# One 1024-wide spectra product, skip term and one block's sums moved to TensorE, quadrant first stages and a tabled order in an S4D and SwiGLU kernel

## The chip, the cores and the metric

The kernel runs on one core of a Trainium2 chip. A core has TensorE (matrix products, PE in the profile), VectorE (DVE), ScalarE (ACT), GpSimd (POOL) and SyncE (SP), which issues most of the DMAs. Each engine works through its own list of instructions in order and waits at semaphores for the others. The metric is the time of one execution on the device in microseconds, lower being better.

## What is computed

x has 2048 positions and 640 channels. The first half convolves a normalised x along its positions with a kernel K that is generated from 128 complex exponentials per channel; the second half is a gated feed-forward. What matters of the reference:

```python
P = jnp.exp((A * dt[:, None])[:, :, None] * pos[None, None, :])
K = 2.0 * jnp.einsum("dn,dnl->dl", C, P).real
Kf = jnp.fft.rfft(K, L2)                      # L2 = 4096
Uf = jnp.fft.rfft(u_t, L2)
y = jnp.fft.irfft(Uf * Kf[None, :, :], L2)[:, :, :L]
return y + u * D_skip[None, None, :]
...
h = _layernorm(x, axis=-1) * (1 + ca) + sa
x = x + ga * _A_ref(h, ...)
h = _layernorm(x, axis=-1) * (1 + cb) + sb
x = x + gb * _B_ref(h, B_w1, B_w3, B_w2)      # silu(h w1) * (h w3), then w2
```

## The kernel before

The channels are taken in five blocks b of 128. All matrix products of the convolution are in fp32, each of them two instructions of TensorE, and an FFT of 4096 points is written as two stages of small products. For each block the kernel does this:

- **The generator**, eight chunks c of 16 channels (`gen_tasks`, `gen_chunk`). GpSimd adds phases (ph) and multiplies tables of exponentials (yy, xx; the tables are in the tiles e of even blocks and `late` of odd ones). ScalarE takes the sines into PSUM (tr). VectorE multiplies the two (five operations, 512 or 1024 wide). TensorE multiplies xx and yy into kps, 32 products of 64 columns. ScalarE copies kps into ks, and VectorE then adds the skip term D_skip (tile dsk) to one column in 64 of it, a 128x4 operation (`skip`). kps has two halves of one PSUM bank, taken in turn.
- **The normalised input** (`h_tasks`): four tiles hn are made by ScalarE or VectorE (four 128x128 operations each), multiplied and added to by VectorE (hb), and sent through DRAM (hs) into xb.
- **The first stage**, of xb and of ks (`first_tasks`): 8 groups each of 8 products of 128 rows and 128 moving columns, into the PSUM tile ps; ScalarE or VectorE copies it into the spectrum sp (or sp2). The constant matrix wk is zero outside two blocks of 64 rows by 64 columns.
- **The spectra** (`spectra_tasks`), 8 steps i: TensorE makes fh and fk, the second stages of the input and of the kernel, in PSUM. ScalarE copies fh into hz (SBUF). VectorE multiplies fk by the real part of hz into the tile fp (SBUF), and by the imaginary part into fk itself, in place (PSUM), 512 wide each. Two 256-wide operations then subtract and add the second product from and to the first (`both`: fp is input and output, fk the other input). After two steps the inverse stage fz is two products with wz for each half f, copied into zt by ScalarE or VectorE and stored to DRAM (zd).

A fifth block's spectra are followed by the tail: the last inverse stage of the first half (iz, izb, loaded from zd; iy, iyb on TensorE), the second normalisation, and the feed-forward, which runs from about 400 us to the end, in fp32r products.

**The order.** Each piece of work is a task that `Plan.add` registers with its engine (or two, the first being preferred), its assumed duration, the tasks that it follows, and the buffers that it takes and gives. `Plan.place` (from line 188) simulates the engines with these durations and a rank per task, read from the table RANKS, and the instructions are then emitted in the order of that simulation. The flag `port` marks tasks that the simulation keeps from running on VectorE and GpSimd at once. Nothing but this emitted order and the waits decides what runs when. The feed-forward (`ffn`, `groups`, `late`) is emitted after the plan, by plain loops.

**Lines.** In the trace most of the plan's instructions are put down to L157, a helper's line, so groups are told apart by the tiles' names.

Of the kernel before, what the change touches and what calls it, by code (L numbers as in the profile page):

```python
# [29 lines left out]
EXPS = ((0, 0, 0, 64.0), (0, 1, 0, 1.0), (1, 0, 0, 512.0), (1, 1, 4, 8.0), (1, 2, 0, 8.0))  # L30
# [3 lines left out]
RANKS = """  # L34
# [65 lines left out]
"""  # L100
FP = 2
EPS = 1e-5
MAGIC = 1.5 * 2.0 ** 23
REV = float(2 ** 32 - 256)
# [2071 lines left out]
```

## Time and profile before

| | before |
|---|---|
| median of 3 runs | 972.96 us (972.6 to 973.78) |
| the profiled execution | 972.31 us |
| its span, first to last instruction | 970.5 us |
| PE busy | 859.9 us, 89% |
| DVE busy | 702.0 us, 72% |
| ACT busy | 546.4 us, 56% |
| POOL busy | 340.5 us, 35% |
| mean granted TensorE clock | 0.975 |

A group's row reads: line, engine, operation, output and inputs by the program's names, shapes, count | busy time, mean of one in ns | the engine's idle time just before them, and what ended it. A row of the timeline reads: start and duration in us, engine, line, operation, count, and in brackets the idle time before it with what ended it. A row of the stretches gives busy times (and counts) of PE, PE's weight loads, DVE, ACT and POOL, then the granted clock, the DMA engines' busy share and GB/s. The shares of the table are averages over stages of different kinds.

### The profile page before, as it was taken

How to read it: one execution, taken by the hardware profiler on the slowest of the kernel's cores; microseconds unless marked ns; L12 is line 12 of the kernel's file. 1: busy time of each engine (PE TensorE's matmuls, PEld its weight loads, DVE VectorE, ACT ScalarE, POOL GpSimd, SP SyncE). 2: the span in 40 equal slices, each digit the busy share in tenths (PEclk: the TensorE clock that was granted, in tenths of full speed). 3: DMA queues.
4: the chain of work that ended last, by engine and by line, in shares of the span. 5: the costliest groups of instructions: out<-in, count | busy, mean ns of one | idle time of the engine just before them, and what ended most of it. 6: DMA issues, size and time to landing. Idle time of an engine off the chain costs nothing.

```text
span 970.5 us, 20551 instructions
## 1 busy us (share of the span) xinstructions
PE 859.9 (89%) x7985; PEld 681.8 (70%) x7985; DVE 702.0 (72%) x1395; ACT 546.4 (56%) x1022; POOL 340.5 (35%) x371
## 2 busy tenths in 40 slices
PE   1464787889899997899999999999999999999997
PEld 1132665767778884677777778888788888888775
DVE  7998899999999968886767677557456464645422
ACT  6877788979888851564434455346444344443412
POOL 1797889879799600002111111000011212120000
PEclk9996999999999999799999999999999999999999
DMA  9955453723425268935434422276342322220374
GB/s 218 275 168 191 111 136 95 177 66 106 111 80 152 74 159 206 241 118 182 122 120 139 122 96 68 82 209 194 112 134 64 102 77 86 82 82 28 108 220 133
DMA packets 110506, 127.31 MB, mean 131 GB/s; under 512 B 10568, under 2 KB 90696, under 8 KB 109128
## 3 DMA queue, kind: packets, MB, share of 16 engines
q1 hardware_dynamic: 109032, 125.21, 45.3%
q8 instruction: 63, 1.03, 0.5%
q10 hardware_dynamic: 1376, 0.79, 0.3%
q14 instruction: 35, 0.29, 0.1%
HBM read 95.82 MB, written 30.15 MB: 130 GB/s over the span
## 4 chain that ended last, share of the span: by engine, by line
PE 70%; DVE 17%; ACT 5%; issue 4%; DMA 3%; POOL 1%; SPq 1%; ACTq 0%; DVEq 0%
PE c L157 19%; PE acc L157 18%; PE X L157 12%; PE ps L157 4%; PE gu L157 3%; DVE yy L157 3%; PE kps L157 3%; PE fz L157 2%; PE fk L157 2%; DVE fp L157 2%; PE fh L157 2%; DVE hn L157 2%; DVE xx L157 2%; DVE xb L157 1%; ACT tr L157 1%
## 5 line engine op out<-in xcount | busy, mean ns | idle before, releaser
L157 PE MATMUL acc<-ah,w 128*128 128x512 f32 x560 | 173.2, 395 | 2.4 <-DMA w<-w2d 1.7
L157 PEld LDWEIGHTS acc<-ah,w 128*128 128x128 f32 x560 | 103.7, 188 | 26.4 <-issue 2.1
L157 PE MATMUL acc<-al,w 128*128 128x512 f32 x260 | 102.4, 394 | 0.0
L665 DVE TENSOR_TENSOR wl<-s,wh 128x256 fp32r<-128x256 f32 x92 | 38.9, 423 | 67.5 <-ACT wh L664 67.1
L841 POOL TENSOR_TENSOR s<-wr 128x256 f32<-128x256 f32 x22 | 16.4, 744 | 187.8 <-DMA wr<-in_w 94.8
L157 POOL TENSOR_TENSOR ph<-p,p 128x1024 int32<-128x1024 int32 x40 | 79.2, 1979 | 8.2 <-ACT tr L157 8.0
L664 ACT ACTIVATE wh<-s 128x256 fp32r<-128x256 f32 x92 | 37.6, 410 | 78.5 <-PE X L157 58.1
L157 PE MATMUL kps<-yy,xx 128*32 128x64 f32 x2560 | 51.8, 234 | 28.6 <-DVE xx L157 21.4
L157 DVE TENSOR_TENSOR yy<-yy,tr 128x512 f32<-128x512 f32 (+1 forms) x80 | 75.3, 943 | 1.2 <-ACT tr L157 0.6
L157 PEld LDWEIGHTS kps<-yy,xx 128*32 128x32 f32 x2560 | 45.1, 116 | 38.3 <-issue 22.0
L664 ACT ACTIVATE wh<-wr 128x256 fp32r<-128x256 f32 x92 | 38.4, 418 | 56.0 <-PE X L157 42.3
L842 POOL TENSOR_TENSOR s<-s,wr 128x256 f32<-128x256 f32 x22 | 16.6, 755 | 134.0 <-issue 133.9
L902 ACT ACTIVATE t<-g 128x512 f32<-128x512 f32 x44 | 27.8, 632 | 52.7 <-DVE g L866 52.7
L157 ACT ACTIVATE tr<-ph,hpi 128x512 f32<-128x512 f32 x80 | 54.6, 690 | 4.4 <-DVE xx L157 2.7
L157 PEld LDWEIGHTS acc<-al,w 128*128 128x128 f32 x260 | 48.9, 188 | 10.8 <-DVE al L665 0.3
L871 DVE SCALAR_TENSOR_TENSOR g<-t,g 128x512 f32<-128x512 f32 x48 | 33.7, 702 | 31.3 <-ACT t L902 29.3
L157 POOL TENSOR_TENSOR yy<-e,e 128x512 f32<-128x512 f32 x48 | 52.4, 1109 | 8.8 <-PE kps L157 5.9
L157 DVE TENSOR_TENSOR xx<-tr,xx 128x512 f32<-128x512 f32 x80 | 54.3, 680 | 1.1 <-ACT tr L157 1.1
L157 PE MATMUL ps<-wk,ks 128*64 128x128 f32 x640 | 42.4, 285 | 13.6 <-DVE ks L157 8.9
L157 ACT ACTIVATE tr<-ph 128x512 f32<-128x512 int32 x80 | 47.3, 598 | 12.4 <-DVE yy L157 6.5
L157 PE MATMUL ps<-wk,xb 128*64 128x128 f32 x640 | 46.1, 295 | 6.3 <-ACT sp L157 3.0
L157 PEld LDWEIGHTS ps<-wk,ks 128*64 128x64 f32 x640 | 37.0, 143 | 20.3 <-ACT hn L157 6.6
(448 smaller groups left out, 2379.7 us busy)
## 6 DMA issues: line engine op xcount, KB each, us to landing
w<-w2d SPq DMA_DIRECT2D x42, 640.0 KB, 3.9
wr<-in_w SPq DMA_DIRECT2D x50, 320.0 KB, 3.9
zd<-zt SPq DMA_DIRECT2D x40, 256.0 KB, 2.9
w2d<-w SPq DMA_DIRECT2D x14, 640.0 KB, 3.5
xs<-in_x SPq DMA_DIRECT2D x16, 320.0 KB, 11.3
hs<-hb SPq DMA_DIRECT2D x20, 256.0 KB, 2.5
xb<-hs SPq DMA_DIRECT2D x20, 256.0 KB, 4.9
iz<-zd SPq DMA_DIRECT2D x32, 160.0 KB, 5.0
```

The source lines that it names most:

```text
L157: self.prev = self.k.order(f(*a, **kw), self.prev)
L664: self.nc.scalar.activation(H, v, AF.Copy)
L665: eng.tensor_tensor(Lo, v, H.bitcast(F32), op=ALU.subtract)
L841: eng.tensor_tensor(s[0], u[:, 0:2], u[:, 2:4], op=ALU.add)
L842: eng.tensor_tensor(s[1], s[0], g[:, 0:2], op=ALU.subtract)
L871: V.scalar_tensor_tensor(g, th, 1.0, g, op0=ALU.add, op1=ALU.mult)
L902: tanh = lambda o, i: A.activation(o, i, AF.Tanh, scale=0.5)
```

## The change

- **The product of the spectra** is one 1024-wide operation: fk (PSUM), read twice, times hz (SBUF), into the four planes of a tile fp twice as large. fk is not written to any more.
- **The sums** of blocks 1 to 4 (SUMS) stay two 256-wide operations of VectorE, now between planes of fp. Block 0 has none: its inverse stage has four products for each half instead of two, with a third column of wz for the minus sign.
- **The skip term** is a product of TensorE, the identity by dsk, added to kps. VectorE's `skip` is gone. kps is one buffer.
- **The first stages** use only the two blocks of wk that aren't zero: 4 groups each of 32 products of 64 rows and 64 columns, by row half h and real or imaginary part r, into two PSUM banks, and two copies of each group.
- **The al8 product** (b by j) is written into a part of the table e itself, and the exponentials end in place.
- **Loads.** The tiles of the first inverse rows (iz0, iz1) lie in sp2 and no longer wait for the memory change behind the generator.
- **The order** is a table, ORDER: entry n is the n-th task that the plan adds, and a mark (') takes its second engine. `Plan.place` is gone. Many assumed durations are changed, which has no effect now that nothing simulates them.

```diff
+SUMS = (1, 2, 3, 4)
...
-    wz = np.tile(np.stack([np.block([c, s]), np.block([-s, c])], 1), (2, 1, 1))
+    wz = np.tile(np.stack([np.block([c, s]), np.block([-s, c]), np.block([-c, -s])], 1), (2, 1, 1))
...
-    def place(self, rank):
+    def sequence(self):
...
+        for x in ORDER.split():
+            n = names[int(x.rstrip("'"))]
...
+            out.append((engs[x.endswith("'")], n))
...
+            nc.tensor.matmul(kps.rearrange("p (e b) -> p e b", b=64)[:, :, 63], self.ident, self.dsk[:, d0 // P, d0 % P // 4:d0 % P // 4 + 4],
+                             start=False, stop=True, skip_group_check=True)
...
-        def skip(c):
-            o = slice(4 * c, 4 * c + 4)
-            V.tensor_add(self.ks[b][:, o, 63], kps.pop(c).rearrange("p (e b) -> p e b", b=64)[:, :, 63], self.dsk[:, b, o])
...
-            for e in range(4):
-                x = self.ks[b][:, 4 * i + e, :] if m else xb[:, :, 4 * i + e]
+            for e in range(8):
+                x = self.ks[b][:, 8 * i + e, :] if m else xb[:, :, 8 * i + e]
                 for r in range(2):
...
-                    nc.tensor.matmul(o, x, self.wk[:, r, :], start=True, stop=True, tile_position=(0, 64 * r))
+                    for h in range(2):
+                        g = slice(64 * h, 64 * h + 64)
+                        o = pk[i, h][r * 64:(r + 1) * 64].rearrange("p (v j i f) -> p i j v f", j=2, i=8, f=2)[:, e]
+                        nc.tensor.matmul(o, x[g], self.wk[g, r, g], start=True, stop=True, tile_position=(64 * h, 64 * r))
...
-            k = bank[1, i]
-            to = k if r else prod[i // 2][:, :, i % 2 * 2:i % 2 * 2 + 2, :].rearrange("p r q d -> p q r d")
-            nc.vector.tensor_mul(to, k, bc(held[i][:, :, r], 2, 2))
+            k = bank.pop((1, i)).rearrange("p q r d -> p r (q d)")
+            h = held[i].rearrange("p q r d -> p r (q d)")
+            to = prod[i // 2][:, :, :, i % 2 * 2:i % 2 * 2 + 2, :].rearrange("p s r q d -> p s r (q d)")
+            nc.vector.tensor_mul(to, bc(k, 1, 2), bc(h, 2, 2))
...
-                p = prod[i // 2][:, r, i % 2 * 2:i % 2 * 2 + 2, :]
-                nc.vector.tensor_tensor(p, p, k[:, :, 1 - r], op=op)
+                nc.vector.tensor_tensor(p[:, 0, r], p[:, 0, r], p[:, 1, 1 - r], op=op)
...
+            terms = ((0, 0, 0), (0, 1, 1), (1, 1, 2), (1, 0, 1))[:2 if last else 4]
...
-            if b == 0:
-                x[0] = self.ks[0].rearrange("p e b -> p (e b)")[:, :1024]
-            else:
-                x[0] = self.xsp.tile([P, 4 * D], F32, name="xs_al8", tag="xs", bufs=4)[:, :1024] if b == 1 else self.fpool.tile([P, 1024], F32, name=f"al8{b}", tag="al8", bufs=1)
-            x[0] = x[0].rearrange("p (d j) -> p d j", j=8)
+            x[0] = E[0][:, :, 1, :]
...
+            t = s[:, :2048] if u == 0 else s[:, 2048:] if u == 1 else self.xb if u == 3 else self.ip.tile([P, 2048], F32, name="iz2")
```

More of the change, by code (lines that the diff above doesn't have):

```diff
@@ L168 @@
 class Plan:
-    LAG = dict(PE=0.2, DVE=0.18, ACT=0.2, POOL=0.15, SP=0.0)
-    CHAIN = dict(DVE=0.12, ACT=0.12, POOL=0.07)
-    NEAR, RATE, LAND, FLY, ISSUE, AWAY, TABLE = 0.1, 235e3, 1.3, 0.7, 0.06, 8, 1.28
     def __init__(self, **rings):
@@ L258, in place @@
+        taken, done, out = {r: [] for r in self.n}, set(), []
+        for x in ORDER.split():
+            n = names[int(x.rstrip("'"))]
+            engs, _, _, after, _, _, take, give, _, _ = T[n]
+            assert n not in done and done.issuperset(after), n
+            for r, y, _ in take:
+                i = len(taken[r]) - self.n[r]
+                assert i < 0 or not uses[r, taken[r][i]], n
+                taken[r].append(y)
             for k in give:
                 uses[k] -= 1
-                given[k] = max(fin + self.LAG.get(e, 0.0), given.get(k, 0.0))
@@ L261, in place @@
-                if not uses[k]:
-                    freed[k] = given[k]
-            for m in nexts[n]:
-                left[m] -= 1
-                if not left[m]:
-                    ready.append(m)
-        assert len(end) == len(T), ("never", [n for n in T if n not in end][:20])
-        return order
-    def run(self):
-        T = self.tasks
-        found = [int(x) for x in RANKS.split()]
-        searched = [n for n in T if n not in self.own]
-        assert len(found) == len(searched)
-        self.order = self.place({n: t[4] for n, t in T.items()} | dict(zip(searched, found)))
-        for s, f, e, n in self.order:
-            if T[n][2]:
-                T[n][2](e)
+            done.add(n)
@@ L282 @@
+            out.append((engs[x.endswith("'")], n))
+        assert len(done) == len(T)
+        return out
+    def run(self):
+        for e, n in self.sequence():
+            if self.tasks[n][2]:
+                self.tasks[n][2](e)
 class K:
@@ L1113, in dst @@
                         return z[u][pr][h * 64:h * 64 + 64]
-                    load(f"iz{u}.{pr}{h}", zv[:, t0:t0 + 2, :cut], dst, 262144, done + ([f"hh{b4}.{i}.m" for i in range(8)] if u > 2 else []))
+                    load(f"iz{u}.{pr}{h}", zv[:, t0:t0 + 2, :cut], dst, 262144, done + ([f"hh{b4}.{i}.m" for i in range(4)] if u > 2 else []),
+                         "inv" if u < 2 else "change")
         def load_up(m):
@@ L1169, in lo @@
                     self.low(h[:, :k], l[:, :k], x)
-                add(f"wh{m}.{i}", "ACT", .36, hi, names + (after[i:i + 1] if after else []), rank)
-                add(f"wl{m}.{i}", "DVE", .42, lo, [f"wh{m}.{i}"], rank)
+                add(f"wh{m}.{i}", "ACT", .32, hi, names + (after[i:i + 1] if after else []), rank)
+                add(f"wl{m}.{i}", "DVE", .34, lo, [f"wh{m}.{i}"], rank)
         def down_split(m, rank):
@@ L1175, in hi @@
                 w2[m] = self.w2_high(m, w2r[m])
-            add(f"w2h{m}", "ACT", .73, hi, [f"ld{m}.{i}" for i in range(1 if m < 13 else 2)], rank, take=[("w2", 1)])
-            add(f"w2l{m}", "DVE", .82, lambda: self.w2_low(m, w2r[m], w2[m]), [f"w2h{m}"] + (["ln1"] if m in (0, 13) else []), rank)
+            add(f"w2h{m}", "ACT", .66, hi, [f"ld{m}.{i}" for i in range(1 if m < 13 else 2)], rank, take=[("w2", 1)])
+            add(f"w2l{m}", "DVE", .74, lambda: self.w2_low(m, w2r[m], w2[m]), [f"w2h{m}"] + (["ln1"] if m in (0, 13) else []), rank)
             add(f"w2k{m}", "SP", 0, lambda: self.w2_keep(m, w2[m]), [f"w2l{m}", "izb1"], rank, dma=[655360],
@@ L1237, in prepare @@
             add(f"iyb{b}", "PE", 1.9, lambda: last_inv(b), [f"izb{b}", f"lwd{b}", "border"] + (["iyb0"] if b else []), 16.0, take=[("gu", 1)])
-            add(f"iab{b}", "DVE", .7, lambda: last_plus(b), [f"iyb{b}"] + [f"lx{b}.{q}" for q in range(4)], rank, give=[("gu", f"iyb{b}"), ("w2", f"izb{b}")])
-            add(f"isb{b}", "DVE", 1.15, lambda: last_stats(b), [f"iab{b}"], rank)
+            add(f"iab{b}", "DVE", .6, lambda: last_plus(b), [f"iyb{b}"] + [f"lx{b}.{q}" for q in range(4)], rank, give=[("gu", f"iyb{b}"), ("w2", f"izb{b}")])
+            add(f"isb{b}", "DVE", .78, lambda: last_stats(b), [f"iab{b}"], rank)
             steps = {}
@@ L1587, in inv @@
             self.sp2 = self.fpool.tile([P, 16, P, 2], F32, name="sp2")
-        plan.add("inv", None, 0, inv, ["cols", "mag1"], 0)
+        plan.add("inv", None, 0, inv, ["cols", "mag1", "hscalef", "colsf", "q0.v1", "q1.v1"] + [f"h0.{i}.a" for i in range(4)] + [f"k0.{i}.e{h}" for i in range(2) for h in range(2)] +
+                 [f"rw{g}" for g in range(4)], 0)
         self.early_tasks(e)
@@ L1613, in border @@
             self.x2 += [self.fp.tile([P, 4, D], F32, name=f"x2{i}") for i in (2, 3)]
-        plan.add("change", None, 0, change, [f"g{b}.7.p", f"g{b}.7.d"] + [f"h{b}.{i}.x" for i in range(4)], 0, own=True)
+        plan.add("change", None, 0, change, [f"g{b}.7.p", f"g{b}.7.r"] + [f"h{b}.{i}.x" for i in range(4)], 0, own=True)
         self.tail_tasks(border, cut)
@@ L1787, in gen_tasks @@
                     give=[("tr", n + f"s{(0, 0, 1, 3, 4)[i]}")])
-            add(n + "p", "PE", 1.1, lambda c=c: ch[c][4](), [n + f"m{i}" for i in range(5)], t + 3,
+            add(n + "p", "PE", 1.28, lambda c=c: ch[c][4](), [n + f"m{i}" for i in range(5)] + (["dsk"] if b == 0 else []), t + 3,
                 take=[("kg", 1)], give=[("yy", n + "z0"), ("xx", n + "z2")])
-            add(n + "r", "ACT", .27, lambda c=c: rows(c), [n + "p"] + ([f"k{b - 1}.{i}.m" for i in range(8)] if b else ["exp0", "q0.t0", "q1.t0"]), t + 3, give=[("kg", n + "p")])
-            add(n + "d", "DVE", .1, lambda c=c: skip(c), [n + "r"] + (["dsk"] if b == 0 else []), t + 3, give=[("kg", n + "p")])
+            add(n + "r", "ACT", .27, lambda c=c: rows(c), [n + "p"] + ([f"k{b - 1}.{i}.m" for i in range(4)] if b else ["exp0", "q0.t0", "q1.t0"]), t + 3, give=[("kg", n + "p")])
     def h_tasks(self, b):
@@ L1803, in h_tasks @@
             place = (lambda: self.pbank("hn")) if b else (lambda: self.psg.tile([P, 512], F32, name="hn", tag="f", bufs=3))
-            add(n + "n", ("ACT", "DVE"), (1.95, .85), lambda e, i=i, place=place: self.h_norm(b, i, place(), e), [n + "l", "hscale"], t, take=[(bank, 1)],
+            add(n + "n", ("ACT", "DVE"), (1.89, 1.66), lambda e, i=i, place=place: self.h_norm(b, i, place(), e), [n + "l", "hscale"], t, take=[(bank, 1)],
                 give=[("xq", n + "l")] if b else [])
@@ L1855, in spectra_tasks @@
         bank, prod, held = {}, {}, {}
-        four = lambda x: x.rearrange("p (q r d) -> p q r d", q=2, r=2)
+        last = b in SUMS
+        four = lambda x: x.rearrange("p (r q d) -> p q r d", q=2, r=2)
         def of(m, i):
@@ L1911, in spectra_tasks @@
             j = 4 * b + i // 2 - FP
[L1912 to L1913 removed]
+            first = [f"hh{b}.{x}.e{h}" for x in range(4) for h in range(2)] + (["wb", "cols", "inv"] if b == 0 else [])
+            firstk = [f"k{b}.{x}.e{h}" for x in range(4) for h in range(2)]
             if i or b == 0:
@@ L1925, in spectra_tasks @@
             j = i // 2
+            y = "c" if last else "x"
             n = f"z{b}.{j}."
-            add(n + "z", "PE", 1.95, lambda j=j: inverse(j), [f"w{b}.{i - 1}.c", f"w{b}.{i}.c"], t + W["late"], take=[("bank", 1), ("bank", 1, "'")],
-                give=[("fp", f"w{b}.{i - 1}.x0")])
+            add(n + "z", "PE", 1.85 if last else 3.63, lambda j=j: inverse(j), [f"w{b}.{i - 1}.{y}", f"w{b}.{i}.{y}"], t + W["late"], take=[("bank", 1), ("bank", 1, "'")],
+                give=[("fp", f"w{b}.{i - 1}.x")])
             for f in range(2):
@@ L1951, in exps @@
                 A.activation(E[t][:, :, m, :], x[0][:, :, k:k + n], AF.Exp, scale=-s)
-        add(f"al8{b}", ("POOL", "DVE"), (1.9, 1.13), begin, [f"al{min(b, 1)}"] + (["inv"] if b > 1 else []) + ([f"exp{b - 1}"] if b > 1 else ["turn1"] if b else []), t, port=True,
-            take=[("xs", 1)] if b == 1 else [])
-        add(f"exp{b}", "ACT", 3.46, exps, [f"al8{b}"] + ([f"g{b - 2}.7.z{i}" for i in range(3)] if b > 1 else ["turn1"] if b else []), t, table="exp",
-            give=[("xs", f"al8{b}")] if b == 1 else [])
+        add(f"al8{b}", ("POOL", "DVE"), (1.9, 1.13), begin, [f"al{min(b, 1)}"] + ([f"exp{b - 1}"] + [f"g{b - 2}.{c}.z{i}" for c in (5, 6, 7) for i in range(3)] if b > 1 else ["turn1"] if b else []), t, port=True)
+        add(f"exp{b}", "ACT", 3.46, exps, [f"al8{b}"], t, table="exp")
         add(f"mag{b}", ("POOL", "DVE"), (1.07, .62), lambda e: self.eng(e).tensor_tensor(E[1][:, :, 0], E[1][:, :, 0], bc(self.mag[:, b], 2, 4), op=ALU.mult),
@@ L2035, in early_tasks @@
         for b in range(4):
-            add(f"x{b}", "SP", 0, lambda b=b: load_xs(b), [], next(lp), dma=[327680] * 4, take=[("xs", 1)])
+            add(f"x{b}", "SP", 0, lambda b=b: load_xs(b), [], next(lp), dma=[360000] * 4, take=[("xs", 1)])
         for k in range(5):
@@ L2086, in scale @@
             self.h_rs = self.rsqrt(self.gp, self.h_ss, NJ, "h", (self.h_nm, 1.0), 1.0 / D, [t[:, i * NJ:(i + 1) * NJ] for i in range(2)])
-        add("hscale", "DVE", 6.5, scale, [f"mean{b}" for b in range(4)] + [f"sq{b}{j}" for b in range(4) if b not in W["stat_v"] for j in range(4)], W["stat"](4), take=[("f2", 1)])
+        add("hscale", "DVE", 5.5, scale, [f"mean{b}" for b in range(4)] + [f"sq{b}{j}" for b in range(4) if b not in W["stat_v"] for j in range(4)], W["stat"](4), take=[("f2", 1)])
         add("hscalef", None, 0, None, ["hscale"], give=[("f2", "hscale")])
@@ L2095, in rows_begin @@
             A.activation(m[:96, 384:], pm[0][:96, 384:], AF.Copy)
-        add("m", "ACT", .9, rows_begin, ["mr4"], 20, take=[("hz", 4)])
+        add("m", "ACT", .6, rows_begin, ["mr4"], 20, take=[("hz", 4)])
         pr = {}
@@ L2117, in fold @@
             V.tensor_mul(self.rB, self.rB, self.rows[2])
-        add("fold", "DVE", 1.6, fold, [f"rw{g}" for g in range(4)], 22, port=True)
+        add("fold", "DVE", 3.2, fold, [f"rw{g}" for g in range(4)], 22, port=True)
         add("wb", "SP", 0, lambda: nc.sync.dma_start(self.wb, self.t_wb), ["fold", "mr4", "lat1", "turn1"], 60, dma=[2097152])
```

227 lines of the change are left out of this document (99 added, 128 removed), and 85 rows, old and new, of tables (ORDER, RANKS).

## The prediction

> **What bounds the kernel now.** I first cut the span into stretches where the load changes: the first chunk of the kernel generator on GpSimd (34.6 us), the start of the generator's third block (160), its last instruction (336.5), the end of the last inverse product (376), and 440, from where only code that the diff leaves alone runs. The columns are the busy times of PE, PE's weight loads, VectorE, ScalarE and GpSimd, with instruction counts, the granted clock, the DMA share and GB/s.
>
> ```profile
> 34.60:160.00 125.40, 83.28 (x1548) 59.66 (x1542) 117.73 (x211) 99.93 (x176) 111.68 (x107) 0.90 0.57 161
> 160.00:336.50 176.50, 156.93 (x3238) 132.08 (x3236) 168.71 (x314) 146.77 (x251) 155.32 (x151) 0.97 0.41 108
> 336.50:376.00 39.50, 38.33 (x604) 30.61 (x602) 28.98 (x60) 19.20 (x38) 0.00 (x1) 1.00 0.66 169
> ...
> 440.00:970.50 530.50, 520.77 (x2323) 415.03 (x2321) 304.31 (x602) 224.60 (x455) 64.91 (x87) 1.00 0.38 115
> ```
>
> The last 530 us are TensorE's (521 of 530.5) and move as a block: the change can only bring their start forward or back. From 34.6 to 336.5 VectorE is the bound: 94% and then 96% busy. GpSimd is next, 89% and 88%. TensorE has room in the first stretch and about 20 us in the second, and is the bound from 336.5 to 376, when GpSimd is done.
>
> Second, VectorE's groups by shape: what the edits touch.
>
> ```profile
> L157 DVE TENSOR_TENSOR yy<-yy,tr 128x1024 f32<-128x1024 f32 x40 | 48.4, 1210 | 0.9 <-ACT tr L157 0.6
> L157 DVE TENSOR_TENSOR fp<-fp,fk 128x256 f32<-128x256 f32 x80 | 29.7, 411 | 0.2
> ...
> L157 DVE TENSOR_SCALAR hn<-xq,rs_y_h,rs_n_h 128x128 f32<-128x128 f32 x44 | 18.1, 412 | 1.2
> ...
> L157 DVE COPY sp<-ps 128x512 f32<-128x512 f32 x20 | 13.4, 683 | 3.2 <-PE ps L157 3.1
> L157 DVE COPY zt<-fz 128x512 f32<-128x512 f32 x9 | 6.2, 685 | 2.2 <-PE fz L157 2.1
> L157 DVE TENSOR_TENSOR ks<-kps,dsk 128x4 f32<-128x4 f32 x40 | 6.0, 157 | 9.8 <-ACT ks L157 5.6 <-PE kps L157 3.1 <-ACT hn L157 1.1
> ```
>
> These ends overlap the next start, so where VectorE is dense an operation costs its distance to the next one. The timeline in the spectra of block 2 gives it:
>
> ```profile
> 224.82 1.21 DVE L157 TENSOR_TENSOR yy<-yy,tr 128x1024 f32<-128x1024 f32 x1
> 225.95 0.69 DVE L157 TENSOR_TENSOR fp<-fk,hz 128x512 f32<-128x512 f32 x1
> 226.55 0.15 DVE L157 TENSOR_TENSOR ks<-kps,dsk 128x4 f32<-128x4 f32 x1
> 226.62 0.69 DVE L157 TENSOR_TENSOR fk<-fk,hz 128x512 f32<-128x512 f32 x1
> 227.22 0.68 DVE L157 TENSOR_TENSOR fp<-fk,hz 128x512 f32<-128x512 f32 x1
> 227.82 0.74 DVE L157 TENSOR_TENSOR fp<-fp,fk 128x256 f32<-128x256 f32 x2
> 228.48 0.69 DVE L157 TENSOR_TENSOR fk<-fk,hz 128x512 f32<-128x512 f32 x1
> ```
>
> So a 512-wide product costs 0.60, a 1024-wide one 1.13, the pair of 256-wide sums 0.66 and the skip add 0.07 us.
>
> **The change part by part, on VectorE.** A step of the spectra now costs 0.60 + 0.60 + 0.66 = 1.86. In block 0 it becomes 1.13, a gain of 0.73 x 8 = 5.8 us. In the other blocks, 1.13 + 0.66 = 1.79 if the sums stay at their price, a gain of 0.07 a step (1.7 for the 24 steps of blocks 1 to 3). The skip add goes: 0.07 x 40 = 2.8 us, and the waits ahead of it, 9.8. The order table also moves evictions; I counted its entries. Normalisations of blocks 1 to 4 on VectorE: 5 instead of 11 (44/4), -6 x 4 x 0.41 = -9.9. First-stage copies 32 instead of 20, inverse copies 10 instead of 9: +13 x 0.60 = +7.8. Net -2.1. ScalarE gets about 11 us of normalisations for 8 of copies, with 147 of 176.5 busy: hidden.
>
> **The sums' new price.** Today each sum has one input in PSUM (fk). Afterwards both terms lie in the SBUF tile fp, in blocks 1 to 4. Does that matter? The trace has VectorE operations with two SBUF inputs, alone and beside GpSimd:
>
> ```profile
> 11.60 1.22 DVE L157 TENSOR_TENSOR ks<-al,j 128x1024 f32<-128x1024 f32 x1
> ...
> 31.53 0.68 DVE L157 TENSOR_TENSOR e<-e,mag 128x512 f32<-128x512 f32 x1
> ...
> 33.06 0.79 DVE L157 TENSOR_TENSOR xb<-late 128x512 f32<-128x512 f32 x1
> ...
> 33.88 3.57 DVE L157 SCALAR_TENSOR_TENSOR wb<-xb,wb 128x512 f32<-128x512 f32 x2
> ...
> 37.38 1.55 DVE L157 TENSOR_TENSOR late<-late 128x512 int32<-128x512 int32 x1
> ...
> 39.45 0.95 DVE L157 SCALAR_TENSOR_TENSOR wb<-late,wb 128x512 int32<-128x512 int32 x1
> ...
> 40.92 0.95 DVE L157 SCALAR_TENSOR_TENSOR xb<-late,xb 128x512 int32<-128x512 int32 x1
> ...
> 43.71 1.54 DVE L157 SCALAR_TENSOR_TENSOR xb<-xb,dt 128x512 f32<-128x512 f32 x1
> ```
> ```profile
> 88.51 2.83 DVE L157 TENSOR_TENSOR xs_al<-al,j 128x1024 f32<-128x1024 f32 x1
> ...
> 98.62 1.72 DVE L157 TENSOR_TENSOR late<-late,mag 128x512 f32<-128x512 f32 x1
> ```
> ```profile
> 88.31 1.95 POOL L157 TENSOR_TENSOR ph<-p,p 128x1024 int32<-128x1024 int32 x1
> ```
>
> The same operation takes 1.22 us at 11.60, with GpSimd idle, and 2.83 at 88.51, where GpSimd's phase add holds until 90.26: 90.26 + 1.2 is its end. It waits for GpSimd's instruction and then runs at full speed. The seven single ones shown from 33.06 on cost 0.11, 0.87, 0.27, 0.27, 0.86, 1.61 and 1.04 over their free 0.68 or 1.22: 0.72 on average. The two in a row at 33.88 cost 3.57 against 1.28, that is 2.3 more. The operations with one input in PSUM, all those of the third fence, show none of it at equally dense GpSimd.
>
> So I price a pair of sums at 2 x 0.72 = 1.4 us more, between 0.6 (two of the cheaper 0.27 ones) and 2.3 (the row of two). A narrow sum waits no less than a wide operation, for what it waits for is GpSimd's instruction. It meets this in blocks 1 to 3, whose spectra run while GpSimd generates the next block: 24 pairs, +33.6 us of VectorE (14 to 55). Block 4's run after 336.5, GpSimd idle: free.
> [...]
>
> **On the other engines.**
>
> ```profile
> 226.85 1.16 PE L157 MATMUL kps<-yy,xx 128*32 128x64 f32 x64
> 227.94 1.99 PE L157 MATMUL fz<-fp,wz 64*128 64x512 f32 x8
> ```
> ```profile
> 329.00 3.14 PE L157 MATMUL ps<-wk,xb 128*64 128x128 f32 x48
> ...
> 346.32 3.71 PE L157 MATMUL ps<-wk,ks 128*64 128x128 f32 x64
> ```
> ```profile
> 103.50 1.05 PE L157 MATMUL pv<-ident,mc 128*128 128x4 f32 x8
> ```
>
> First stages: instead of 32 instructions of 128 columns, 64 of 64 columns in four quadrants do the same. The nearest row is the generator's product: 64 columns, four column groups, 64 instructions in 1.09 us, 17 ns each. At that price a quarter of the kernel's stage falls from 1.85 to 1.1; at today's 58 ns an instruction it would rise to 3.7. I take 1.1: the column groups show that separate parts of the array overlap. The stage of h reads its weights 32 elements apart (65 ns an instruction, 3.14/48): I leave it at today's 2.1, between 1.1 and 4.2. On the path lies only what follows the last product: half the kernel's stage of block 4, 3.71 now, 2 x 1.1 then: -1.5.
> [...]
> The skip product is two more instructions with 4 columns behind each of 40 products: 2 x 1.05/8 = 0.26, some 10 us that TensorE's idle time hides; uncovered only behind the last product, +0.3. Block 0's inverse doubles, +1.99 x 4 = 8 us, in the first stretch, where TensorE idles 42; if it weren't hidden, +8. One buffer kg for two: the next product comes microseconds later, so 0, or up to 0.4 x 40 where it queues behind ScalarE.
>
> **Start and end.**
>
> ```profile
> 10.25 0.83 DVE L157 TENSOR_TENSOR late<-late,dt 128x640 f32<-128x640 f32 x1 [2.96 <-DMA late<-in_a_im]
> ```
> ```profile
> PE iyb L157 <- DMA izb<-zd: 4.4, 3, 1.8
> ```
>
> The table puts block 0's al8 product (11.60 now) third on VectorE, into the 2.96 us wait for a_im: -1.1. Loads of the first two inverse rows no longer wait for the generator's end; of the last rows' 4.4 us wait for DMA I take 1 off (0 to 4.4).
>
> **The sum.** Start -1.1. First stretch: VectorE 117.7 - 5.8 - 16 x 0.07 = 110.8; GpSimd has 111.7 plus one multiply of mag moved to it, so about 113 and a few waits, 116 for 125.4: -9.4. Second stretch: -1.7 (skip) - 1.7 (products) - 2.1 (evictions) + 33.6 (sums), and of 7.8 us idle 2.8 less, as a later VectorE waits less: +25. End: -1.5 + 0.3 - 1 = -2.2. In all +12.4 on the profiled span of 970.5, 982.9; that run took 972.31, 1.8 more than its span, and lies 0.65 under the median: 985. With the pair at 0.6 the sum is -7 (966), at 2.3 it is +34 (1007).
>
> **Rivals.** (1) Faster: GpSimd is rarely in the way. Once VectorE is late, GpSimd stands still for want of yy and xx buffers, and a sum finds it idle. For it: GpSimd already idles 21 us of the second stretch. Against: after the change it has the same work, 155 us in some 200, so three sums in four still meet it. At no price the second stretch is 8.3 shorter and the whole 21 us: 952. It decides from a pair under (33.6 - 12.4)/24 = 0.9 us. (2) The quadrants' weight loads don't overlap: the first stages double, 2 us more for each of some 32 units from 160 on, 64 us against 20 idle and the 25 by which VectorE is late: 20 beyond the forecast, 1005. Against it the 17 ns row. (3) Terms cancel near a pair of 0.9: 973, no change.
>
> **How the numbers follow.** Forecast, the sums meet GpSimd: 0.50, by itself 976 to 1000 (pair 1.0 to 2.0). Rival 1: 0.38; rival 2: 0.05; rival 3: 0.07. A measurement of this kernel tells 0.2% (2 us) from no change. Slower 0.55, faster 0.38, same 0.07. The range takes rival 1 in nearly whole and leaves out the tops: 954 to 1002.
>
> **What would show it.** Right: fp sums over 0.8 us on average in blocks 1 to 3 and about 0.41 in block 4; GpSimd's own instructions longer beside them; the generator's last instruction after 350 us; first-stage kernel bursts of 64 in 1.1 us. Wrong: sums at 0.41 throughout and the generator's end at 315 to 320, or a generator bound by waits for TensorE.

## The result, and the profile after

The changed kernel takes 1002.34 us (median of 4 runs, 999.51 to 1005.72) against 972.84 (4 runs, 972.6 to 973.78): a ratio of 1.0303, 95% interval 1.027 to 1.0336. Slower was the likelier forecast; its 985 us is 17 too low, and the range's upper end, 1002, lies just under the time. The profiled execution took 1005.72 us with a span of 1003.9, so 33.4 us are to be found between the two profiles.

The same stretches as before (busy time of PE, its weight loads, VectorE, ScalarE, GpSimd, then clock, DMA share, GB/s):

```profile
34.60:160.00 125.40, 86.94 (x1714) 63.56 (x1716) 109.00 (x180) 101.20 (x185) 101.10 (x98) 0.81 0.56 166
160.00:336.50 176.50, 149.36 (x3766) 123.87 (x3766) 161.71 (x212) 132.43 (x225) 144.91 (x141) 0.94 0.36 92
336.50:376.00 39.50, 33.30 (x959) 26.77 (x956) 34.60 (x45) 26.82 (x49) 23.36 (x19) 0.96 0.39 104
376.00:440.00 64.00, 51.27 (x466) 37.38 (x460) 46.52 (x131) 20.47 (x38) 0.63 (x1) 0.87 0.77 184
```

Everything is later, and the two engines that set the pace before are less dense: VectorE has 109 of 125.4 us in the first stretch (117.7 before) and 162 of 176.5 in the second (169), GpSimd 101 (112) and 145 (155). They wait for other engines more. Where the time went is read from the first phase add of each block of the generator, and from the last inverse product (timelines of GpSimd and PE; first the kernel before, then the changed one):

```profile
97.83 1.95 POOL L157 TENSOR_TENSOR ph<-p,p 128x1024 int32<-128x1024 int32 x1
160.14 1.96 POOL L157 TENSOR_TENSOR ph<-p,p 128x1024 int32<-128x1024 int32 x1
...
373.19 1.99 PE L157 MATMUL fz<-fp,wz 64*128 64x512 f32 x8 [1.17 <-DVE fp L157]
```
```profile
28.85 2.28 POOL L149 TENSOR_TENSOR ph<-p,p 128x1024 int32<-128x1024 int32 x1
...
104.39 1.95 POOL L149 TENSOR_TENSOR ph<-p,p 128x1024 int32<-128x1024 int32 x1
170.63 1.96 POOL L149 TENSOR_TENSOR ph<-p,p 128x1024 int32<-128x1024 int32 x1
...
405.70 1.99 PE L149 MATMUL fz<-fp,wz 64*128 64x512 f32 x8
```

The generator starts 5.8 us sooner (34.62 before), but block 1 starts 6.6 later and block 2 10.5 later. From block 2's start to the last inverse product it takes 235.1 us instead of 213.1, 22.0 more. Behind that product the two differ by 0.9 (1003.9 - 405.70 against 970.5 - 373.19). So the loss is 10.5 + 22.0 + 0.9 = 33.4.

**The sums.** VectorE's groups by shape, and a piece of the timeline of GpSimd and VectorE in the spectra of block 1, then of VectorE in those of block 4:

```profile
L149 DVE TENSOR_TENSOR fp<-fp 128x256 f32<-128x256 f32 x64 | 50.5, 835 | 0.3
L149 DVE TENSOR_TENSOR fp<-fk,hz 128x1024 f32<-128x1024 f32 x40 | 48.6, 1216 | 12.6 <-PE fk L149 11.6 <-ACT hz L149 0.9
```
```profile
208.32 2.63 DVE L149 TENSOR_TENSOR fp<-fp 128x256 f32<-128x256 f32 x2
208.54 2.13 POOL L149 TENSOR_TENSOR ph<-p,p 128x1024 int32<-128x1024 int32 x1
```
```profile
404.61 0.76 DVE L149 TENSOR_TENSOR fp<-fp 128x256 f32<-128x256 f32 x2
```

A pair takes 0.76 us in block 4, where GpSimd is done. Of the pair at 208.32 the first sum (0.54 us long) is still running when a phase add of GpSimd begins at 208.54, and the second sum ends 0.28 us after that add (208.32 + 2.63 against 208.54 + 2.13). So that second, 256-wide sum took 2.1 us, 1.7 over the 0.41 of before: as much as the 1024-wide product at 88.51 lost in the kernel before (2.83 for 1.22). By blocks the mean of one sum is 1097, 888, 932 and 422 ns: in blocks 1 to 3 972 on average, 0.56 more than the 411 of before, 1.1 a pair.

**TensorE.** Its waits from 28 to 440 us, before and after (waited for; total, times, longest), the rows with no releaser and the nearest others:

```profile
PE kps L157 <- DVE xx L157: 21.4, 9, 12.1
...
PE kps L157 <- issue: 1.4, 2, 0.9
...
PE fh L157 <- issue: 1.3, 1, 1.3
```
```profile
PE kps L149 <- DVE xx L149: 31.3, 17, 8.0
PE ptp L149 <- DVE wb L149: 12.4, 1, 12.4
...
PE kps L149 <- issue: 4.2, 3, 2.1
PE ps L149 <- issue: 4.2, 3, 3.3
...
PE fh L149 <- issue: 2.6, 1, 2.6
```

GpSimd's waits for the generator's product, before and after:

```profile
POOL yy L157 <- PE kps L157: 14.9, 11, 3.9
...
POOL xx L157 <- PE kps L157: 1.0, 1, 1.0
```
```profile
POOL yy L149 <- PE kps L149: 35.4, 15, 4.7
POOL xx L149 <- PE kps L149: 6.3, 3, 3.0
```

They rose from 15.9 to 41.7 us: the generator is now held up by TensorE, which waits for VectorE. And "issue" is time in which the engine waited for nothing that the profile shows: 11.0 us against 2.7. Some of these gaps, in TensorE's timeline:

```profile
116.82 0.42 PE L149 MATMUL kps<-yy,xx 128*32 128x64 f32 x11
119.33 1.92 PE L149 MATMUL kps<-yy,xx 128*32 128x64 f32 x53 [2.08 <-issue]
...
258.29 0.89 PE L149 MATMUL kps<-yy,xx 128*32 128x64 f32 x43
260.97 0.64 PE L149 MATMUL kps<-yy,xx 128*32 128x64 f32 x21 [1.79 <-issue]
...
315.47 0.45 PE L149 MATMUL fh<-sp,wb 128*64 128x128 f32 x4
318.55 0.91 PE L149 MATMUL fh<-sp,wb 128*64 128x128 f32 x12 [2.63 <-issue]
...
374.76 1.38 PE L149 MATMUL ps<-wk,ks 64*64 64x64 f32 x75
379.44 1.76 PE L149 MATMUL ps<-wk,ks 64*64 64x64 f32 x53 [3.30 <-issue]
381.14 1.97 PE L149 MATMUL fh<-sp,wb 128*64 128x128 f32 x16
...
387.68 1.07 PE L149 MATMUL fh<-sp,wb 128*64 128x128 f32 x16
```

They fall into the middle of a burst, at no fixed place of it. The trace's DMA records have a queue of instructions, which moves 16 KB at a time. In each of these gaps such a load ends, and 1.3 to 1.5 us later TensorE goes on:

```
load of 16 KB: start, took     its end    TensorE goes on
116.93  0.96                   117.89     119.33   (+1.44)
258.34  1.35                   259.69     260.97   (+1.28)
315.71  1.38                   317.09     318.55   (+1.46)
376.93  1.06                   377.99     379.44   (+1.45)
```

Counted along TensorE's own list the gaps do have a fixed place. The list has 18,927 instructions (9377 weight loads, as many products and 173 semaphore waits) for the 74 loads of the run: 256 to a load. All seven gaps end where 193 instructions more than a multiple of 256 have started, and so do two of the three in the kernel before (those that end at 254.30 and 304.99 us). So TensorE stands where the instructions of one load are used up. Of the 54 loads up to 440 us, 47 begin when TensorE is already working off the 256 before the ones that they bring, the others at most 1.2 us sooner: in the median 0.95 us after it has begun with them, at the four gaps above 2.3 to 4.0 us after. Why they begin that late there isn't shown.

The whole run's loads of that queue stand on the page (packets, MB, share), before and after:

```profile
q8 instruction: 63, 1.03, 0.5%
```
```profile
q8 instruction: 74, 1.21, 0.5%
```

Behind the 3.30 us gap 16 instructions took 1.97 us, and 1.07 some 6 us later. The granted clock was 0.50 there:

```profile
378.50:385.30 6.80, 5.86 (x93) 5.74 (x94) 1.49 (x3) 1.50 (x3) 0.00 (x0) 0.50 0.96 194
```

The half clock began inside the gap, at 378.5, 2.4 us after TensorE's last product before it (374.76 + 1.38); from 376.2 to 378.5 and from 385.3 to 390 the granted clock was 1.00. What sets it off was not shown.

### The profile page after: what moved, and what is told of

Its sections match the earlier page's. It is cut to its first block, busy times and chain, and to the rows that moved or that the text cites. A ratio compares the mean times of both kernels' runs of the same rounds, so it can differ in the third digit from the quotient of the medians.

```text
span 1003.9 us, 23237 instructions
## 1 busy us (share of the span) xinstructions
PE 880.0 (88%) x9377; PEld 695.6 (69%) x9377; DVE 714.6 (71%) x1285; ACT 551.1 (55%) x1034; POOL 347.9 (35%) x373
## 4 chain that ended last, share of the span: by engine, by line
PE 66%; DVE 15%; ACT 9%; issue 5%; DMA 4%; SPq 1%; POOL 1%; ACTq 0%; DVEq 0%; POOLq 0%
PE c L149 18%; PE acc L149 17%; PE X L149 11%; DVE fp L149 4%; PE gu L149 3%; PE fh L149 3%; PE ps L149 3%; PE fk L149 3%; DVE yy L149 2%; ACT tr L149 2%; PE kps L149 2%; PE fz L149 2%; DVE xx L149 1%; DVE xb L149 1%; PE iy L149 1%
## 5 line engine op out<-in xcount | busy, mean ns | idle before, releaser
L149 DVE TENSOR_TENSOR yy<-yy,tr 128x512 f32<-128x512 f32 x80 | 75.5, 945 | 5.0 <-ACT tr L149 4.1
L149 ACT ACTIVATE tr<-ph,hpi 128x512 f32<-128x512 f32 x80 | 54.2, 688 | 10.3 <-DVE yy L149 6.3
L149 DVE TENSOR_TENSOR fp<-fk,hz 128x1024 f32<-128x1024 f32 x40 | 48.6, 1216 | 12.6 <-PE fk L149 11.6
L149 PE MATMUL fz<-fp,wz 64*128 64x512 f32 x192 | 52.0, 643 | 6.0 <-DVE fp L149 3.9
L149 PE MATMUL fh<-sp,wb 128*64 128x128 f32 x640 | 48.7, 299 | 8.7 <-DVE fp L149 3.6
```

Source lines behind the costliest of these rows:

```text
L149: self.prev = self.k.order(f(*a, **kw), self.prev)
```

## The experiments

Theories: **A**, the sums held up by GpSimd; **B**, the order of the table; **C**, TensorE starved of instructions by the quadrants. All ratios are against the kernel before, with 95% intervals.

**e1 and e2, order and operations crossed.** e1 has the changed operations in the order of the kernel before, e2 the old operations in the new order, each task at the place of its namesake.

> All operations of the changed kernel, but in the order in which the kernel before issued its tasks (each task stands where its namesake stood; a first-stage unit of two banks where the second of its two former units stood). Theory A (the sums, held up by GpSimd, are what costs): the order changes little, 990 to 1005 us, and the 256-wide sums still average over 0.7 us. Theory B (the table's order makes the engines wait for one another): most of the 29 us comes back, 965 to 982 us, whatever the sums take.

> The reverse: all operations of the kernel before (512-wide products, sums with one term in PSUM, skip add on VectorE, 128-row first stages), issued in the order of the new table. Theory A: 965 to 980 us, since no sum has two SBUF inputs. Theory B: 992 to 1010 us, with GpSimd again waiting some 40 us for products of TensorE.

1043.45 us (1.0687 to 1.0757) and 1029.61 (1.0558 to 1.0607): both worse than either kernel. Neither theory's number came. It seems that an order fits its own operations; with others, engines wait at other places (TensorE's gaps in e1: 15.0 us; none in e2). For the whole time the cross doesn't tell an order's worth. For the generator's block 0 it does: by the first phase adds of blocks 0 and 1 it lasts 75.5 us in the changed kernel and 75.1 in e2 (28.79 to 103.92), 63.2 in the kernel before and 63.4 in e1 (33.58 to 96.99). Its length goes with the order, whatever the operations are.

**e3 and e4, the sums.** e3:

```diff
-                add(n + "c", "DVE", .67, lambda i=i: both(i), [n + "x"], t - q)
+                add(n + "c", "DVE", .67, None, [n + "x"], t - q)
```

e4 has this line too, and

```diff
-            k = bank.pop((1, i)).rearrange("p q r d -> p r (q d)")
+            k = bank.pop((1, i))
+            if last:
+                p = prod[i // 2][:, 0, :, i % 2 * 2:i % 2 * 2 + 2, :]
+                nc.vector.tensor_mul(p.rearrange("p r q d -> p q r d"), k, bc(held[i][:, :, 0], 2, 2))
+                nc.vector.tensor_mul(k, k, bc(held[i][:, :, 1], 2, 2))
+                for r, op in enumerate((ALU.subtract, ALU.add)):
+                    nc.vector.tensor_tensor(p[:, r], p[:, r], k[:, :, 1 - r], op=op)
+                return
+            k = k.rearrange("p q r d -> p r (q d)")
```

> The changed kernel without the 256-wide sums of blocks 1 to 4 (the second term of each spectrum product is left out there); order and all else as they are. It bounds what the sums can cost in all. Theory A: VectorE loses 50 us of work in its dense stretches, 950 to 970 us. Theory B: the waits stay, and it gives back under 15 us, 987 to 1000 us.

> The changed kernel with the sums of blocks 1 to 4 as before the change: two 512-wide products, the second left in PSUM, and the pair of sums reading it there, directly behind the products. Theory A: the sums fall from 0.84 to about 0.41 us each, 27 us less on VectorE against 2 us more for the products, 975 to 985 us. Theory B: the sums fall as well, but the kernel stays within 10 us of the changed one, 992 to 1002 us.

978.92 us (1.0037 to 1.0101) and 985.25 (1.0096 to 1.0166). VectorE's groups in e4:

```profile
L149 DVE TENSOR_TENSOR fp<-fp,fk 128x256 f32<-128x256 f32 x64 | 24.1, 418 | 1.1
```

With one term in PSUM the same sums take 418 ns in the mean of all four blocks, three of them beside GpSimd (972 ns there with both in SBUF), and 17.1 us come back; 985.25 lies just above A's 975 to 985. That these sums cost some 17 us in this order is shown. But even with the sums left out (e3, which also takes away the 24 us that they cost anyway) the kernel isn't back at 973: e3 lies between the numbers of A and of B, and something else costs nearly as much.

**e5 and e7, the first stages.** e5 is the changed kernel with

```diff
+            for h in range(2):
+                for e in range(4):
+                    x = self.ks[b][:, 8 * i + 4 * h + e, :] if m else xb[:, :, 8 * i + 4 * h + e]
+                    for r in range(2):
+                        o = pk[i, h][r * 64:(r + 1) * 64].rearrange("p (v j i f) -> p i j v f", j=4, i=4, f=2)[:, e]
+                        nc.tensor.matmul(o, x, self.wk[:, r, :], start=True, stop=True, tile_position=(0, 64 * r))
```

in place of the 64 products by quadrants, and the evictions to match; e7 has this and e4's edit.

> The changed kernel with the first stages in their old form: 128-row products, 32 instructions of 128 columns for a unit of two banks instead of 64 of 64 columns; order, evictions and sums as changed. Theory C (twice the instructions of TensorE: it stands still while the next 16 KB of its instructions arrive, 11 us of gaps with no releaser against 2.7 before): the gaps fall below 4 us and 5 to 10 us come back, 992 to 997 us, although each unit of the kernel's stage takes 0.75 us longer. Rival (the gaps lie beside other waits, the shorter units pay): 1002 to 1008 us.

> Both undone at once: the sums read PSUM and the first stages have 128 rows. If the two costs add up (17 us for the sums, 5 to 10 for the gaps), 975 to 981 us. If they cover one another, 983 to 987 us.

990.99 us (1.0177 to 1.0232) and 969.01 (0.9964 to 0.9997; 10 runs). The quadrants cost 11.3 us with the new sums and 16.2 without them, the sums 22.0 without the quadrants: together 33.3, which is more than the whole loss. e7 lies below both of its numbers, so the two costs do more than add up; it is about 3 us faster than the kernel before (972.03 in the same round), and its interval ends just under 1. e5 is 1 us better than theory C had. In e5 and e7 TensorE has no gap without a releaser left, and the page counts ten loads fewer than after the change (e7):

```profile
q8 instruction: 64, 1.05, 0.5%
```

The quadrants issue 32 x 40 = 1280 instructions for products more, each with its weight load, with ten loads more: 128 such pairs to a load.

That the quadrants bring the gaps and cost these times is shown; that the gaps are the whole cost isn't. With them the granted clock is lower too: over the span 0.963 to 0.966 in the runs of e4, 0.972 to 0.980 in those of e7. e4 has 13.4 us of gaps. How its 16.2 us divide between the gaps and the slower clock was not measured.

**e6, two buffers for the generator's product**, the halves of one bank:

```diff
-                kps[c] = self.psg.tile([P, 256], F32, name=f"kps{b}{c}", tag="kg", bufs=1)
+                if b == c == 0:
+                    self.kg = self.psg.tile([P, 2, 256], F32, name="kps", tag="kg", bufs=1)
+                kps[c] = self.kg[:, c % 2]
```

> The changed kernel with the two alternating halves of one PSUM bank for the generator's product, as before the change, instead of one buffer; order as changed. If the single buffer holds the next product back behind ScalarE's row copy, up to 0.4 us for each of 40 products: 988 to 998 us. Otherwise unchanged: 1000 to 1004 us.

1003.53 us (1.0289 to 1.0365): no difference. The forecast's 0 for this edit holds.

**e8, block 0 in the old order.**

> The changed kernel with only the first 343 tasks of the table (those up to the generator's first chunk of block 1) put into the order that the kernel before had for them, the rest of the table as it is. The generator's block 0 took 75.5 us after the change and 63.2 before. If that order is the reason, block 1 starts some 5 to 10 us sooner than at 104.4 and the kernel gains as much, 992 to 998 us. If it is the operations or a later wait, 1000 to 1008 us.

1013.45 us (1.0395 to 1.0467), above both numbers. Its generator:

```profile
98.33 1.95 POOL L151 TENSOR_TENSOR ph<-p,p 128x1024 int32<-128x1024 int32 x1
...
176.22 1.95 POOL L151 TENSOR_TENSOR ph<-p,p 128x1024 int32<-128x1024 int32 x1
```

Block 1 does start 6.1 us sooner, so the new order makes block 0 that much later. But then block 1 takes 77.9 us instead of 66.2. Presumably what the new order did in block 0 is missing there; which work that is was not traced.

**e9, e14 and e15, number or pace.** e9 is e7 with

```diff
-                        nc.tensor.matmul(o, x, self.wk[:, r, :], start=True, stop=True, tile_position=(0, 64 * r))
+                        for c in range(2):
+                            nc.tensor.matmul(o[:, 2 * c:2 * c + 2], x, self.wk[:, r, 64 * c:64 * c + 64], start=True, stop=True, tile_position=(0, 64 * r))
```

e14 and e15 are e7 with quadrants in the kernel's stage alone (`if m == 1`) and in that of h alone (`if m == 0`).

> The kernel of e7 (sums from PSUM, 128-row first stages), with each 128-column product of the first stages issued as two of 64 columns on the same 128 rows: as many TensorE instructions as with the quadrants, without the quadrants. Theory C (the number of instructions is what starves TensorE): some 55 loads of 16 KB of instructions again, gaps without a releaser of 8 to 14 us, 978 to 990 us, near the 985 of e4. Rival (it was the quadrants): no gaps, 968 to 974 us.

> The kernel of e7 with quadrants for the kernel's first stage alone (units of 64 instructions in 1.1 us, 17 ns each); the stage of h keeps 128 rows. If fast bursts outrun the loading of instructions, nearly all the gaps return, 7 to 13 us of them, and 978 to 986 us. If the total number of instructions is what matters, half of them: 3 to 6 us, 973 to 978 us.

> The kernel of e7 with quadrants for the stage of h alone (units of 64 instructions in 2.2 us, 34 ns each); the kernel's stage keeps 128 rows. Bursts theory: under 3 us of gaps, 967 to 972 us. Number theory: 3 to 6 us of gaps, 973 to 978 us.

1008.35 us (1.0354 to 1.0389), 972.87 (0.9971 to 1.001) and 975.38 (1.0005 to 1.004). TensorE's waits in e14, then in e15, and a unit of h in e9's timeline of PE:

```profile
PE ps L149 <- issue: 5.4, 2, 3.0
```
```profile
PE kps L149 <- issue: 2.7, 2, 1.9
...
PE ps L149 <- issue: 0.8, 2, 0.6
```
```profile
341.30 4.28 PE L149 MATMUL ps<-wk,xb 128*64 128x64 f32 x64
```

By 128 pairs to a load five more loads each than in e7, 5.4 and 3.5 us of gaps, +3.9 and +6.4 us. (From round to round the kernel before moved between 971.85 and 973.91, so a difference from e7 in another round is good to some 2 us.) Both gaps and both times lie at the number theory's values, and the bursts theory, which put nearly all on the fast kernel's stage, falls. But the times don't follow the gaps, and together they are 10.3 of the 16.2 us that both stages cost. e9 has the 1280 products more, by that count all ten loads, but only 2.7 us of gaps and lies above both of its numbers. There 64 instructions of h take 4.3 us instead of 2.2, and 64 of the kernel's stage 2.1 instead of 1.2. For the 20 units of h alone that is some 42 us more than in e7 (2.1 each), as much as the whole 39: that work rather than the loading makes it slow. So in these runs number and pace both count (5.4 us of gaps where a unit of quadrants takes 1.16 us, 3.5 at 2.24, 2.7 at e9's 2.1 and 4.3): gaps come where a load's instructions are used up faster than the next load arrives.

**e10, e7's operations in the old order**, and **e11, no sums on VectorE at all** (e5 with e3's line and this one):

```diff
-            terms = ((0, 0, 0), (0, 1, 1), (1, 1, 2), (1, 0, 1))[:2 if last else 4]
+            terms = ((0, 0, 0), (0, 1, 1), (1, 1, 2), (1, 0, 1))
```

> The operations of e7 in the order of the kernel before (as in e1). What it differs from the kernel before by is then the skip term and block 0's sums on TensorE, first-stage units of two banks and the single buffer of the generator's product. If the new table is worth anything by itself, this is slower than e7: 975 to 990 us. If the old order is better, with block 0's generator some 10 us shorter, 955 to 967 us.

> The kernel of e5 (128-row first stages) with the partial sums of all blocks made by TensorE, as in block 0: no 256-wide sums, 8 us more of TensorE in each of blocks 1 to 4. VectorE loses 24 + 6 us against e7, TensorE gains 32. If TensorE's room hides that, 955 to 965 us; if TensorE then sets the pace of blocks 1 to 4, 970 to 990 us.

1004.65 us (1.0302 to 1.0343): slower still than expected, the old order doesn't fit these operations either. 989.74 (1.0161 to 1.0191) for e11. Its second stretch, by the same columns as above:

```profile
160.00:336.50 176.50, 171.83 (x3216) 138.35 (x3214) 135.32 (x178) 136.54 (x232) 147.42 (x145) 1.00 0.34 90
```

TensorE is busy for 172 of 176.5 us at full clock: it has become the bound there.

**e12 and e13, block 0's sums and the skip term back on VectorE**, each on e7. e12, then e13 (which also leaves out TensorE's skip product):

```diff
-            if last:
+            if True:
...
-            terms = ((0, 0, 0), (0, 1, 1), (1, 1, 2), (1, 0, 1))[:2 if last else 4]
+            terms = ((0, 0, 0), (0, 1, 1), (1, 1, 2), (1, 0, 1))[:2]
```
```diff
-            A.activation(self.ks[b][:, 4 * c:4 * c + 4, :], kps.pop(c).rearrange("p (e b) -> p e b", b=64), AF.Copy)
+            k = kps.pop(c).rearrange("p (e b) -> p e b", b=64)
+            o = slice(4 * c, 4 * c + 4)
+            A.activation(self.ks[b][:, o, :], k, AF.Copy)
+            V.tensor_add(self.ks[b][:, o, 63], k[:, :, 63], self.dsk[:, b, o])
```

> The kernel of e7 with block 0's sums on VectorE too (from PSUM, as before the change) instead of doubled inverse products. Cost sum of the forecast: VectorE +5.8 us in the first stretch, TensorE -8 us. If VectorE sets that stretch, 972 to 976 us; if TensorE's 8 us were not hidden after all, 962 to 967 us; if both are covered, 967 to 971 us.

> The kernel of e7 with the skip term as before the change: a 4-column add on VectorE behind ScalarE's row copy instead of two products of TensorE. Forecast: 2.8 us of VectorE and some 10 us of waits ahead of it come back, 972 to 982 us. Rival: TensorE's two products cost as much on the path from generator to buffer, 965 to 971 us.

974.07 us (0.9988 to 1.0026) and 990.08 (1.0135 to 1.0199). Block 0's sums on TensorE are worth 5.1 us by the medians, and 3 by the ratios. The skip term is worth 21, outside both numbers, in this order: in e13 its adds have

```profile
L149 DVE TENSOR_TENSOR ks<-kps,dsk 128x4 f32<-128x4 f32 x40 | 6.5, 162 | 28.0 <-ACT ks L149 27.8
```

6.5 us of work and 28 us of VectorE waiting for ScalarE ahead of them, since each add stands directly behind the copy that it needs. A table with a later place for them was not tried.

**e16, e17 and e18, what fills the first stretch**, each e7 with another table.

> The kernel of e7 with the normalisations of h that the new table puts ahead of the generator's block 2 beyond the old ones (two of block 2, three of block 3, one of block 4), and those behind them, at the chunks of the generator where the kernel before had them. If this moved work is what fills the first stretch, block 2 starts 5 to 9 us sooner than in e7 (163.9 us), and the second stretch is longer by as much: 966 to 974 us. If the first stretch is held up by something else, block 2 starts within 3 us of 163.9.

> The kernel of e7 with the rest of blocks 1 to 4's parameter chain (pc1, q1) 25 places later in the table, so that TensorE makes the generator's first product before it waits for the chain's transposes. If the chain in front is what makes block 0 long (74.0 us in e7), block 1 starts 3 to 6 us sooner than at 102.7 and the kernel gains as much, 962 to 967 us. If not, 967 to 975 us.

> The same with 45 places: the chain's second half behind the products of the generator's first chunk. By the same theory block 1 starts 5 to 10 us sooner, 958 to 966 us; if later steps wait for the parameters instead (the table wb, the products of h), 970 to 985 us.

e16: 1016.73 us (1.0413 to 1.0502). Block 2 starts at 161.51, only 2.4 us sooner than in e7, and block 3 not before 268.87 (225.98 in e7): moving the normalisations, and those behind them, opened single waits of GpSimd for TensorE of 17 and 14 us. e17: 968.51 (0.9931 to 0.9969); TensorE's 12.4 us wait for the parameters is gone (one of 9.8 us for a DMA of in_w_mod came instead), yet block 1 starts at 102.66 as in e7 (102.69), so that wait was not on the path. e18: 977.77 (1.0023 to 1.0055), block 1 at 111.36. So none of the three accounts for the length of block 0. e17 and e7 beat both kernels, by 5 and 3 us against the kernel before in their own rounds, and can't be told apart.

## Why the prediction was right and wrong

The two stretches by their parts. "Forecast" are the prediction's terms, "measured" differences of the starts of block 2 and of the last inverse product in e5, e7, and the two kernels:

| us | forecast | measured |
|---|---|---|
| to block 2's start: quadrants | 0 | +6.2 (170.63 - 164.46, e5) |
| to block 2's start: all else | -10.5 | +4.3 (164.46 - 160.14) |
| from there to the last product: quadrants | -1.5 | +9.5 (235.1 - 225.6, e5) |
| the sums, less the products' gain | +31.9 | +21.0 (225.6 - 204.6, e7) |
| all else | -7.3 with the tail | -8.5 (204.6 - 213.1), tail +0.9 |

Block 2's start in e5, then in e7:

```profile
164.46 1.96 POOL L149 TENSOR_TENSOR ph<-p,p 128x1024 int32<-128x1024 int32 x1
```
```profile
163.91 1.95 POOL L149 TENSOR_TENSOR ph<-p,p 128x1024 int32<-128x1024 int32 x1
```

The forecast's terms add up to +12.6 and not to its +12.4; nothing hangs on that.

**The sums: right, and over-priced.** The marks that the prediction named as "right" came: sums over 0.8 us in blocks 1 to 3 and 0.42 in block 4, the phase adds beside them longer (2.13 us for 1.95), the generator's end after 350 us (its last chunk begins at 363.18). So did one of "wrong": a generator held up by TensorE. The pair cost 1.1 us instead of 1.4, and 21 of its 27 us of VectorE reached the end. Rival 1 fails: GpSimd stood more, but not so often that a pair fell under 0.9.

**The quadrants: the first step that failed.** The prediction counted that 64 instructions of 64 columns last 1.1 us, and they nearly do (1.16 to 1.24 us without a gap), and it set all but the last half stage at nothing, hidden in TensorE's room. It did not ask what twice as many instructions need. They cost 11.3 us, and 16.2 with e4's sums. Rival 2 had the right part of the change, the first stages, and nearly the right total, 1005, by the wrong mechanism, so that is luck: the quadrants' units take less time than before or about as much (1.16 us for 1.85, 2.24 for 2.1), so their weight loads overlap as expected, but the instructions' own loading does not keep up (11.0 us of gaps). In the second stretch this error and the sums' nearly cancel (+30.4 forecast, +30.5 measured).

**The first stretch: the step that made the number wrong.** "VectorE 117.7 - 5.8 - 16 x 0.07 = 110.8 ... -9.4" took VectorE's work as what sets the stretch, and counted the table's tasks by engine over the whole, not by where they stand. The table puts 16 pairs of normalisation multiplications ahead of block 2 instead of 10, some 8 us. VectorE's groups up to block 2's start, before and after:

```profile
L157 DVE TENSOR_TENSOR hn<-hn,rw 128x512 f32<-128x512 f32 x10 | 6.9, 693 | 0.6 <-ACT hn L157 0.6
L157 DVE TENSOR_TENSOR hb<-hn,rw 128x512 f32<-128x512 f32 x10 | 6.8, 679 | 0.0
```
```profile
L149 DVE TENSOR_TENSOR hn<-hn,rw 128x512 f32<-128x512 f32 x16 | 10.9, 693 | 0.6 <-ACT hn L149 0.5
L149 DVE TENSOR_TENSOR hb<-hn,rw 128x512 f32<-128x512 f32 x16 | 10.9, 684 | 0.1
```

The saving itself is real: with block 0's sums put back (e12) block 2 starts at 169.28 instead of 163.91. But up to block 2's start VectorE's work did not fall: 148.1 us in e7, 145.3 in the kernel before. And that work alone is not what sets the stretch. In e16 VectorE has 136.3 us up to block 2, 11.8 less than in e7, and block 2 starts only 2.4 us sooner. The stretch is a chain of products between GpSimd, ScalarE, VectorE and TensorE: 5.1 us of the +4.3 arise in block 0 (102.95 in e5 against 97.83), and e1 and e2 show that block 0's length goes with the order and not with the operations. Which of the order's moves does it stays open: e16 speaks against the moved normalisations as the main cause, e17 against the wait for the parameters.

**The start and the rest.** The generator's start gained 5.8 us instead of 1.1, and block 0's length took it back. The skip term was under-priced: 2.8 us of work and 2.8 of idle time, while e13 has 21 against it, in an order that has no place for it. One buffer for two: nothing, as forecast. The tail's -1 for earlier loads did not come (+0.9).

## What to carry to other kernels

Count instructions as well as their time: splitting the first stages' products made ten loads of instructions more here (74 for 64), and TensorE stopped for up to 3.3 us where a burst used up its loaded instructions, with nothing in the profile but a gap without a releaser and more packets on the instruction queue. Keep one input of a narrow VectorE operation in PSUM while GpSimd is dense (418 ns against 972 here). Price an order by what it puts into each stretch, stretch by stretch, and test an operation's worth inside the order that was made for it.

## What the runs showed of the hardware

One load of 16 KB goes with 128 of TensorE's instructions for products and their weight loads (10 loads more for 1280: 74 in e4, 64 in e7), and after each of the four gaps shown TensorE went on 1.28 to 1.46 us after the load's end. In units of 64 instructions by quadrants of 64 rows, the kernel's stage takes 1.16 us, 18 ns each, and that of h, whose weights are read 32 elements apart, 2.24 us, 35 ns each: a unit of h gained nothing by the quadrants (2.1 us for its 32 before). That the distance is the reason was not tested. Two units in the changed kernel's timeline of PE:

```profile
362.12 2.24 PE L149 MATMUL ps<-wk,xb 64*64 64x64 f32 x64
...
369.30 1.16 PE L149 MATMUL ps<-wk,ks 64*64 64x64 f32 x64
```
